# Fewer single blocks and earlier pairs in an on-chip-routed mixture of experts, with separately anchored scatters

## The chip, the core and the metric

The kernel runs on one core of a Trainium2 chip. Its engines are named as in the profile: PE is TensorE (PEld its weight loads), DVE is VectorE, ACT is ScalarE, POOL is GpSimd, and SP is the engine whose queue issues most loads. The metric is device time in microseconds. A run is given as the median of several executions.

## What is computed

28,672 tokens of 192 channels (8 sequences of 3,584) first go through a causal convolution with 7 taps, whose softmaxed weights are shared by the 24 channels of a head. The result then goes through a mixture of 8 experts with one expert per token. A token takes the expert with the largest logit, or, if its local gate is not below one half, the expert of the token before it.

```
w = softmax(weight)                                   # 8 heads x 7 taps
y[b, s, h] = sum_k w[h, k] * x_pad[b, s + k, h]       # 24 channels per head
logits = y @ w_gate ; local = sigmoid(y @ w_local)
e[s] = argmax(logits[s]) if s == 0 or local[s] < 0.5 else e[s - 1]
out[s] = softmax(logits[s])[e[s]] * (relu(y[s] @ w1[e[s]]) @ w2[e[s]])   # 192 -> 1024 -> 192
```

## The kernel before

**Parts and blocks.** Tokens come in 16 parts of 1,792. For each part, DVE (with eight ACT instructions) convolves, `route` finds each token's expert and place, and POOL scatters the 14 row groups of the part into the DRAM table `slots`, sorted by expert (`put`, L794, its indirect DMA on L801). A unit is 128 such rows of one expert. PE works through blocks of one unit (a single), two units (a pair) or four (a quad), always of one expert, since the 1.5 MB of that expert's weights are loaded once per block. Quads use a seven-product scheme (`seven`, L1136) and can only be formed when all parts are routed.

**The static plan.** How many blocks of each kind exist is fixed when the program is written, from what must be full whatever the routing. `ONE` counts singles after each part up to `EARLY` (L47, 3), `TWO` counts pairs after each later part up to `PAIRED` (L65, 60). With these values there are 35 singles (7 after the first part, 14 more after the second, 14 more after the third), then 60 pairs (3 after the fourth part, 7 more after each part that follows), then 13 quads, 4 pairs and 14 singles. In the loop over blocks (L1359) they run in this order. A spare group behind a conditional takes what is left over.

**A block.** `hidden` (L988) writes the hidden layer to `hps` (L999) and ACT takes it out with a relu (L1004). `turn` (L964) transposes the next block's rows on PE and ACT copies them out (L985). `output` (L1009) multiplies by the second weights into two PSUM tiles `yps` (L1016); ACT scales one half out (L1024), DVE adds the other half (L1030), and POOL scatters each unit's 128 finished rows to the output (L1034). `yps` has two buffers and a block uses both, so the next block's `output` can only begin when this block's L1030 is done.

**The order of the work between.** All engines work in the order of the program text as it is emitted. DVE's convolution and routing is cut into small pieces, and `step(time)` (L1258) emits pieces until their noted costs add up to `time`: routing pieces first, and convolution pieces (0.6 each, L411) from a "hop" on, which is where the next routing piece waits for another engine. A single has steps of 2.1, 1.2 and 1.3 around its output, a pair 4.8, 1.2 and 3.6. `start_conv` (L1229) lets a convolution begin if it is at most two parts ahead of the routing and no scatters of three parts before are left.

**Scatters and rows.** `put(behind)` takes one row group off the list `to_put` and ties its scatter to the instruction given. A single or a pair places two in `hidden`. A pair places one more behind the transposes while more than 7 are left, and one in `output` while more than 12 are left. `ensure(i)` (L1311), called at the head of block i, loads the rows of the blocks up to i + 3. A block of part g can only be loaded when all of g's scatters are emitted. While some are left, it does this:

```
while st["routed"] < g or any(p[0] <= g for p in to_put):
    if j > i + 2:
        return
    step(4.2)
    put()
```

Of the kernel before, what the change touches and what calls it, by code (L numbers as in the profile page):

```python
# [9 lines left out]
I32 = mybir.dt.int32  # L10
Act = mybir.ActivationFunctionType
# [6 lines left out]
P = 128  # L18
B, S, D = 8, 3584, 192
# [3 lines left out]
N = B * S  # L23
UT = 128
NT = 14
# [10 lines left out]
KD = D // DR  # L36
FK = F // P
BT = 2 * UT
KT = BT // P
# [4 lines left out]
CAP = CAPU * UT  # L44
NU = (N + E * (UT - 1)) // UT
DUMMY = E * CAPU
EARLY = 3  # L47
SPARE = 2


def _sure(tokens, size):

    return max(0, -(-(tokens - E * (size - 1)) // size))
# [3 lines left out]
def _likely(tokens, size, left):  # L57
# [4 lines left out]

LAST = NPART - 1
PADS = NPART
PAIRED = 60  # L65
LEFT4 = E * (QT // 2 + UT // 8)
LEFT2 = E * (BT // 2 + UT // 8)
ONE = [_sure(min(g + 1, EARLY) * PT, UT) for g in range(NPART)]
TWO = [min(PAIRED, _sure((g + 1) * PT - ONE[-1] * UT, BT)) if g >= EARLY else 0
       for g in range(NPART)]  # L70
# [13 lines left out]
IX = DG - 1  # L84
# [3 lines left out]
WA = F * KD // 2  # L88
# [8 lines left out]
def bcast_mid(ap, n):  # L97

    return ap.rearrange("p (o a) -> p o a", o=1).to_broadcast([ap.shape[0], n, ap.shape[1]])
# [3 lines left out]
def kernel(  # L103
# [10 lines left out]
    nc = tc.nc  # L114
# [45 lines left out]
    with tc.tile_pool(name="scr", bufs=1) as scr:  # L160
        w = scr.tile([1, H, KC], F32, name="w")
# [164 lines left out]
    slot = early[:, (H + 4) * TB:(H + 4) * TB + UT]  # L326
# [6 lines left out]
    rows = cst.tile([Q, 2, Q], F32, name="rows")  # L333
# [18 lines left out]
    for zero in (rk, bk, mk, mc, tq):  # L352
# [8 lines left out]
                      in_=bcast_mid(pad, KQ))  # L361
# [15 lines left out]
    def halves():  # L377
        return [(half, slice(half * DR, (half + 1) * DR)) for half in range(2)]
# [410 lines left out]
    to_put = []  # L789
    puts = []  # L790
    waited = set()
    SYNC = mybir.DependencyInfo(mybir.DependencyClass.Sync, mybir.DependencyReason.DATA)

    def put(behind=None):  # L794


        if not to_put:
            return
        g, rows, to = to_put.pop(0)
        nc.gpsimd.nop()  # L800
        ins = nc.gpsimd.indirect_dma_start(  # L801
            out=slots[:, :], in_=rows, in_offset=None,
            out_offset=bass.IndirectOffsetOnAxis(ap=to, axis=0)).ins
        if behind is not None:
            tc.add_manual_dep(ins, behind.ins.name, SYNC, reason="scatters apart")
        if puts:
            tc.declare_no_dep(ins, group="puts", reason="slots of their own")
        if g:
            tc.declare_no_dep(ins, group="gets", reason="those slots were full before")
        puts.append((g, ins))  # L810
        tc.add_to_no_dep_group("puts", ins)
        tc.add_to_no_dep_group(f"puts{g}", ins)
# [175 lines left out]
    def hidden(n, wb, xT, shares=(1, 1)):  # L988
        hT = hp.tile([P, FK, BT], F32, name="hT")
        w = slice(0, n * P)  # L990


        for two in range(2):
            hps = [hps_p.tile([P, 2, BT], F32, name="hps") for half in range(2)]
            for d in range(KD):
                for j in range(2):
                    f0 = (d * 4 + two * 2 + j) * P
                    for half, rows in halves():
                        nc.tensor.matmul(hps[half][:, j, w], lhsT=wb[rows, f0:f0 + P],  # L999
                                         rhs=xT[rows, d, w], start=(d == 0 and j == 0),  # L1000
                                         stop=(d == KD - 1), skip_group_check=True)
            for half in range(2):
                m = half * 4 + two * 2
                relu = nc.scalar.activation(hT[:, m:m + 2, w], hps[half][:, :, w], Act.Relu)  # L1004
            for _ in range(shares[two] if n == KT else (0, sum(shares))[two]):
                put(relu)
        return hT

    def output(n, wb, xg, hT):  # L1009

        yps = [yps_p.tile([P, 512], F32, name="yps") for half in range(2)]
        for m4 in ([0, 1, 4, 5], [2, 3, 6, 7]):
            for k in range(n):
                for m in m4:
                    for half, rows in halves():
                        nc.tensor.matmul(yps[half][:, k * D:(k + 1) * D],  # L1016
                                         lhsT=hT[rows, m, k * P:(k + 1) * P],
                                         rhs=wb[rows, WA + m * D:WA + (m + 1) * D],
                                         start=(m == 0 and k == 0), stop=(m == FK - 1),
                                         skip_group_check=True)  # L1020
        o_sb = op.tile([P, KT, D], F32, name="o_sb")
        y = [[yps[half][:, k * D:(k + 1) * D] for half in range(2)] for k in range(n)]
        for k in range(n):
            half = nc.scalar.activation(o_sb[:, k, :], y[k][0], Act.Copy, scale=xg[:, k, 0:1])  # L1024
        if n == KT and len(to_put) > NT - 2:
            put(half)

        step(1.2 if n > 1 or st["block"] else 0)
        for k in range(n):
            nc.vector.scalar_tensor_tensor(o_sb[:, k, :], y[k][1], xg[:, k, 0:1], o_sb[:, k, :],  # L1030
                                           Alu.mult, Alu.add)

            nc.gpsimd.nop()
            sent = nc.gpsimd.indirect_dma_start(  # L1034
                out=out, in_=o_sb[:, k, :], in_offset=None,
                out_offset=bass.IndirectOffsetOnAxis(ap=xg.bitcast(I32)[:, k, IX:], axis=0),
                bounds_check=N - 1, oob_is_err=False)
            tc.declare_no_dep(sent.ins, group="sent", reason="each token has one slot")
            tc.add_to_no_dep_group("sent", sent.ins)


    room = {}
# [215 lines left out]
    def step(time):  # L1258

        start_route()  # L1260
        start_conv()
        go = st["rgen"] is not None
        while time > 0:
            c = route_op() if go else conv_op()
            if c is None:
                if not go:
                    break
                go = False
            elif c == "hop":
                go = False  # L1270
            elif c == "placed":
                pass
            else:
                time -= c
# [10 lines left out]
    def rest(work):  # L1285
        for _ in work:
            pass
# [62 lines left out]
    xT, _ = turn(blocks[0][1], xgs[0])  # L1350
# [8 lines left out]
    for i, (_, n, _, _) in enumerate(blocks):  # L1359
        st["block"] = i  # L1360
        ensure(i)
        weights(i + AHEAD)
        if i == LATE:
            x_in[3] = load_x(3)
        if i == FIRST - 1:
            make_room()
        n_next = blocks[i + 1][1] if i + 1 < len(blocks) else 0

        def weights_next():
            return combine_w(wbs[i + 1]) if n_next == KQ else iter([None] * 4)  # L1370

        if i < FIRST:
            hT = hidden(n, wbs[i], xT, (1, 1) if i else (0, 0))
            if i < FIRST - 1:
                xT, copied = turn(n_next, xgs[i + 1])
                if len(to_put) > NT // 2 and n == KT:
                    put(copied)
            else:
                wt = list(weights_next())[-1]
                xT, _ = turn_in(n_next, turn_out(n_next, xgs[i + 1]))  # L1380
                xc = combine_x(xT)
            step(2.4 if i == 0 else 2.1 if n == 1 else 4.8)
            output(n, wbs.pop(i), xgs.pop(i), hT)
            if i == 0:
                rest(route1)
            step(1.3 if n == 1 else 3.6)
            continue
        if i == FIRST:
            banks.close()
            for k in range(3):  # L1390
                late_p.append(ctx.enter_context(tc.tile_pool(name=f"late{k}", bufs=1, space=PSUM)))

        def turn_next():
            return turn_out(n_next, xgs[i + 1]) if n_next else None

        if n == KQ:
            hT, at, wt = seven(wbs[i], wt, xT, xc, turn_next, weights_next)
        else:
            hT = hidden_late(n, wbs[i], xT)
            at = turn_next()  # L1400
        if n_next:
            xT, _ = turn_in(n_next, at)
        wts, xcs = [], []

        def rows_next():
            if n_next == KQ:
                xcs.append(combine_x(xT))
            if n == KQ:
                wts.append(next(wt))

        def between(part, two, k, ins):
            if n == KQ and part == 0 and two != k:
                put(ins)
                if k:
                    next(wt)

        output_late(n, wbs.pop(i), xgs.pop(i), hT, rows_next, between)
        if n == KQ:
            wt = wts[0]
        xc = xcs[0] if xcs else None  # L1420
# [89 lines left out]
```

## Time and profile before

| | |
|---|---|
| three runs | 1322.0, 1322.66, 1323.66 us; median 1322.66 |
| profiled execution | 1305.35 us, of which its span 1303.6 us |
| granted PE clock, mean | 0.997 |
| DVE busy | 846.3 us (65%), nearly all of it before 830 us |
| POOL busy | 523.1 us (40%) |
| wb weight loads of 1.5 MB | 122, besides 12 of a third of that |
| last routing result of parts 3, 4, 5 and 16 (DVE, L769) | 104.85, 161.7, 218.5 and 829.6 us |
| first pair's hidden layer (PE) | 252.5 us |

A line of the chain of waits gives start, length and what ran. A line of the timeline gives start, length, engine, line, operation and tiles, and in brackets how long the engine was idle before and what released it. In the list of waits, the numbers are the total, how often, and the longest. A row of windows gives the busy time of each engine in a stretch and its PE clock.

### The profile page before, as it was taken

The page shows a single profiled execution, that of the slowest core. Times are in us where ns is not written, and L with a number is a line of the kernel's source. Part 1 is how long each engine was busy: PE and PEld are TensorE (multiplying, and loading weights), DVE is VectorE, ACT ScalarE, POOL GpSimd, SP SyncE. Part 2 cuts the span into 40 slices and gives each one's busy share as a digit, 9 for nine tenths or more (in the row PEclk, how much of TensorE's full clock was granted, in tenths as well). Part 3 has the DMA queues.
Part 4 walks back from the last instruction along what each step waited for, and adds up shares of the span by engine and source line. Part 5 has one row for each costly group of instructions (what it writes and reads, how often), then busy time and mean ns, then how long its engine had stood idle before and what let it go on. Part 6 is the DMA issues. An engine that isn't in the chain of part 4 may idle for free.

```text
span 1303.6 us, 40830 instructions
## 1 busy us (share of the span) xinstructions
PE 1284.2 (99%) x16434; PEld 1220.6 (94%) x16434; DVE 846.3 (65%) x2526; ACT 651.1 (50%) x1482; POOL 523.1 (40%) x577
## 2 busy tenths in 40 slices
PE   9899999999999999999999999999999999999997
PEld 7799999999999999999999999999999999999997
DVE  5989898988988899998999996801333333330000
ACT  5456565544445445444454544444645556454453
POOL 3455353533435344353544534454433433322211
PEclk9999999999999999999999999999999999999999
DMA  5799999975757576575765755666323323324584
GB/s 195 285 357 415 386 384 345 398 273 202 269 203 278 196 274 244 207 280 190 281 246 204 281 193 205 214 213 235 128 87 135 122 105 140 110 94 167 212 303 164
DMA packets 63077, 300.42 MB, mean 230 GB/s; under 512 B 12064, under 2 KB 34263, under 8 KB 45474
## 3 DMA queue, kind: packets, MB, share of 16 engines
q1 hardware_dynamic: 40560, 252.54, 53.2%
q0 software_dynamic: 22320, 45.22, 9.5%
q8 instruction: 131, 2.15, 0.7%
q14 instruction: 64, 0.52, 0.1%
q10 hardware_dynamic: 2, 0.00, 0.0%
HBM read 252.12 MB, written 46.07 MB: 229 GB/s over the span
## 4 chain that ended last, share of the span: by engine, by line
PE 96%; DVE 3%; issue 0%; POOL 0%; POOLq 0%; ACT 0%; DVEq 0%
PE yps L1016 31%; PE hps L999 31%; PE ps L1196 15%; PE ps L1152 8%; PE ps L1103 4%; PE xps L383 2%; PE xps L1152 2%; PE hps L604 2%; DVE y_sb L411 1%; PE hps L233 1%; PE hps L178 0%; DVE hot L574 0%; PE hps L256 0%; PE yps L264 0%; DVE run L475 0%
## 5 line engine op out<-in xcount | busy, mean ns | idle before, releaser
L1016 PE MATMUL yps<-wb,hT 64*128 64x192 f32 x4960 | 429.8, 325 | 3.2 <-DVE o_sb L1030 2.4
L999 PE MATMUL hps<-xT,wb 64*128 64x256 f32 (+1 forms) x4560 | 425.9, 338 | 1.9 <-DVE at L503 1.2
L999 PEld LDWEIGHTS hps<-xT,wb 64*128 64x128 f32 x4560 | 378.7, 188 | 33.9 <-issue 3.9
L1016 PEld LDWEIGHTS yps<-wb,hT 64*128 64x128 f32 x4960 | 405.7, 187 | 4.6 <-DVE o_sb L1030 2.7
L411 DVE SCALAR_TENSOR_TENSOR y_sb<-x_sb,c,y_sb 128x336 f32<-128x336 f32 x672 | 375.6, 569 | 28.4 <-ACT y_sb L401 10.5
L801 POOL DMA_INDIRECT slots<-y_sb,posi x228 | 229.6, 1007 | 205.7 <-ACT xT L985 90.8
L1004 ACT ACTIVATE hT<-hps 128x512 f32<-128x512 f32 (+1 forms) x380 | 176.4, 516 | 244.5 <-PE hps L999 244.5
L1034 POOL DMA_INDIRECT out_dram<-o_sb,xg x155 | 161.5, 1042 | 276.0 <-DVE o_sb L1030 222.2
L1209 DVE SCALAR_TENSOR_TENSOR o_sb<-ps,y_sb,o_sb 128x192 f32<-128x192 f32 x74 | 28.1, 413 | 233.5 <-ACT o_sb L1206 233.5
L1214 POOL DMA_INDIRECT out_dram<-o_sb,y_sb x74 | 76.4, 1032 | 237.5 <-DVE o_sb L1209 218.7
L1196 PE MATMUL ps<-wb,x_sb 64*128 64x192 f32 x1952 | 165.0, 323 | 0.0
L1196 PEld LDWEIGHTS ps<-wb,x_sb 64*128 64x128 f32 x1952 | 159.3, 187 | 0.6
L1024 ACT ACTIVATE o_sb<-yps,xg 128x192 f32<-128x192 f32 x155 | 58.7, 418 | 178.4 <-PE yps L1016 178.3
L985 ACT COPY xT<-xps 128x256 f32<-128x256 f32 (+3 forms) x380 | 142.0, 374 | 10.6 <-PE xps L383 4.8
L1030 DVE SCALAR_TENSOR_TENSOR o_sb<-yps,xg,o_sb 128x192 f32<-128x192 f32 x155 | 58.6, 410 | 77.2 <-ACT o_sb L1024 77.0
L1206 ACT ACTIVATE o_sb<-ps,y_sb 128x192 f32<-128x192 f32 x74 | 27.9, 418 | 102.2 <-PE ps L1196 97.7
L1152 PE MATMUL ps<-x_sb,wb 64*128 64x256 f32 x624 | 73.7, 376 | 0.0
L1152 PEld LDWEIGHTS ps<-x_sb,wb 64*128 64x128 f32 x624 | 59.0, 187 | 7.3
L401 ACT ACTIVATE y_sb<-x_sb,c 128x336 f32<-128x336 f32 x112 | 61.9, 578 | 0.0
L1103 PE MATMUL ps<-x_sb,wb 64*128 64x128 f32 (+1 forms) x864 | 61.6, 295 | 0.0
L1103 PEld LDWEIGHTS ps<-x_sb,wb 64*128 64x128 f32 x864 | 59.4, 188 | 0.9 <-issue 0.2
L1083 ACT COPY x_sb<-xps 128x128 f32<-128x128 f32 (+5 forms) x124 | 58.7, 473 | 2.3
(277 smaller groups left out, 1043.5 us busy)
## 6 DMA issues: line engine op xcount, KB each, us to landing
wb<-in_w_dram SPq DMA_DIRECT2D x122, 1536.0 KB
x_sb<-in_x_dram SPq DMA_DIRECT2D x14, 1920.0 KB
xg<-slots SPq DMA_DIRECT2D x60, 195.0 KB
wb<-in_w_dram SPq DMA_DIRECT2D x12, 512.0 KB
y_sb<-slots SPq DMA_DIRECT2D x13, 390.0 KB
slots<-y_sb,posi POOLq DMA_INDIRECT x228
xg<-slots SPq DMA_DIRECT2D x33, 97.5 KB
x_sb<-in_xb_dram SPq DMA_DIRECT2D x4, 768.0 KB
```

Of the source, the lines that this page charges most:

```text
L401: nc.scalar.activation(cols(h), chans(h, 0), Act.Copy, scale=c[:, h, 0:1])
L411: nc.vector.scalar_tensor_tensor(cols(h), chans(h, k), c[:, h, k:k + 1], cols(h), Alu.mult, Alu.add)
L801: ins = nc.gpsimd.indirect_dma_start(out=slots[:, :], in_=rows, in_offset=None, out_offset=bass.IndirectOffsetOnAxis(ap=to, axis=0)).ins
L985: copied = nc.scalar.copy(a, b)
L999: nc.tensor.matmul(hps[half][:, j, w], lhsT=wb[rows, f0:f0 + P], rhs=xT[rows, d, w], start=(d == 0 and j == 0), stop=(d == KD - 1), skip_g ...
L1004: relu = nc.scalar.activation(hT[:, m:m + 2, w], hps[half][:, :, w], Act.Relu)
L1016: nc.tensor.matmul(yps[half][:, k * D:(k + 1) * D], lhsT=hT[rows, m, k * P:(k + 1) * P], rhs=wb[rows, WA + m * D:WA + (m + 1) * D], start= ...
L1034: sent = nc.gpsimd.indirect_dma_start(out=out, in_=o_sb[:, k, :], in_offset=None, out_offset=bass.IndirectOffsetOnAxis(ap=xg.bitcast(I32)[ ...
L1103: nc.tensor.matmul(hps[:, half, j, :], lhsT=wb[rows, f0:f0 + P], rhs=xT[rows, d, :], start=(d == 0 and j == 0), stop=(d == KD - 1), skip_g ...
L1152: ins = nc.tensor.matmul(to[:, half, j, :], lhsT=b[rows, j * P:(j + 1) * P], rhs=a[rows, :], start=(first and j == 0), stop=True, skip_gro ...
L1196: ins = nc.tensor.matmul(yps[:, half, k * D:(k + 1) * D], lhsT=h[two][rows, side, j, k * P:(k + 1) * P], rhs=wb[rows, WA + f * D:WA + (f + ...
L1214: sent = nc.gpsimd.indirect_dma_start(out=out, in_=o_sb[:, k, :], in_offset=None, out_offset=bass.IndirectOffsetOnAxis(ap=xg.bitcast(I32)[ ...
```

## The change

`EARLY` becomes 2 and `PAIRED` 63. By the plan's formulas that gives 21 singles (7 and 14), then 63 pairs (3 after the third part, then 7 after each), 15 quads, 4 pairs and 14 singles. The number of units worked on stays 229.

In `hidden`, a single's two scatters are placed one behind each half instead of both behind the second. In `output`, the extra scatter of a pair is tied to a matmul in the middle of the output instead of to the ACT instruction after it. The scatter of a block's second unit is no longer emitted in `output` but kept in a list `held` and emitted in the next block's `hidden`, tied to a matmul there, or, before the first quad, without a tie.

```diff
-EARLY = 3
+EARLY = 2
-PAIRED = 60
+PAIRED = 63
...
                     for half, rows in halves():
-                        nc.tensor.matmul(hps[half][:, j, w], lhsT=wb[rows, f0:f0 + P],
+                        ins = nc.tensor.matmul(hps[half][:, j, w], lhsT=wb[rows, f0:f0 + P],
...
+                        if held and d:
+                            held.pop(0)(ins)
...
-            for _ in range(shares[two] if n == KT else (0, sum(shares))[two]):
+            for _ in range(shares[two]):
                 put(relu)
...
+                if m4[0] and k == 0 and n == KT and len(to_put) > NT - 2:
+                    put(ins)
...
-        if n == KT and len(to_put) > NT - 2:
-            put(half)
...
+            if k == 0:
+                deliver(o_sb, xg, 0)
+            else:
+                held.append(lambda ins, k=k: deliver(o_sb, xg, k, ins))
+
+    held = []
+
+    def deliver(o_sb, xg, k, behind=None):
+
+        nc.gpsimd.nop()
+        sent = nc.gpsimd.indirect_dma_start(
+            out=out, in_=o_sb[:, k, :], in_offset=None,
...
+        if behind is not None:
+            tc.add_manual_dep(sent.ins, behind.ins.name, SYNC, reason="scatters apart")
...
         if i == FIRST:
+            while held:
+                held.pop(0)(None)
```

More of the change, by code (lines that the diff above doesn't have):

```diff
@@ L998, in hidden @@
                     for half, rows in halves():
-                        nc.tensor.matmul(hps[half][:, j, w], lhsT=wb[rows, f0:f0 + P],
-                                         rhs=xT[rows, d, w], start=(d == 0 and j == 0),
-                                         stop=(d == KD - 1), skip_group_check=True)
+                        ins = nc.tensor.matmul(hps[half][:, j, w], lhsT=wb[rows, f0:f0 + P],
+                                               rhs=xT[rows, d, w], start=(d == 0 and j == 0),
+                                               stop=(d == KD - 1), skip_group_check=True)
+                        if held and d:
+                            held.pop(0)(ins)
             for half in range(2):
@@ L1015, in output @@
                     for half, rows in halves():
[L1016 to L1020, printed above, removed]
+                        ins = nc.tensor.matmul(yps[half][:, k * D:(k + 1) * D],
+                                               lhsT=hT[rows, m, k * P:(k + 1) * P],
+                                               rhs=wb[rows, WA + m * D:WA + (m + 1) * D],
+                                               start=(m == 0 and k == 0), stop=(m == FK - 1),
+                                               skip_group_check=True)
+                if m4[0] and k == 0 and n == KT and len(to_put) > NT - 2:
+                    put(ins)
         o_sb = op.tile([P, KT, D], F32, name="o_sb")
@@ L1023, in output @@
         for k in range(n):
-            half = nc.scalar.activation(o_sb[:, k, :], y[k][0], Act.Copy, scale=xg[:, k, 0:1])
-        if n == KT and len(to_put) > NT - 2:
-            put(half)
+            nc.scalar.activation(o_sb[:, k, :], y[k][0], Act.Copy, scale=xg[:, k, 0:1])
         step(1.2 if n > 1 or st["block"] else 0)
@@ L1031, in output @@
                                            Alu.mult, Alu.add)
[L1033 to L1039, printed above, removed]
+            if k == 0:
[7 more added lines that the diff above has]
+            out=out, in_=o_sb[:, k, :], in_offset=None,
+            out_offset=bass.IndirectOffsetOnAxis(ap=xg.bitcast(I32)[:, k, IX:], axis=0),
+            bounds_check=N - 1, oob_is_err=False)
+        if behind is not None:
+            tc.add_manual_dep(sent.ins, behind.ins.name, SYNC, reason="scatters apart")
+        tc.declare_no_dep(sent.ins, group="sent", reason="each token has one slot")
+        tc.add_to_no_dep_group("sent", sent.ins)
     room = {}
```

## The prediction, written before the changed kernel ran

> **What bounds the kernel now.** I read the page first: engines, then slices.
>
> ```profile
> PE 1284.2 (99%) x16434; PEld 1220.6 (94%) x16434; DVE 846.3 (65%) x2526; ACT 651.1 (50%) x1482; POOL 523.1 (40%) x577
> ...
> DVE  5989898988988899998999996801333333330000
> ```
>
> PE is never free for long. DVE is nearly full for the first 24 slices (782 us) and mostly at a third or less after 850 us, so only before that can DVE work push PE. The chain of waits gives each kind of block its period, from one block to the next of its kind.
>
> ```profile
> 98.16 2.68 PE hps L999 x48
> 103.61 2.68 PE hps L999 x48
> 109.05 2.68 PE hps L999 x48
> ...
> 263.47 5.18 PE hps L999 x48
> ...
> 274.13 5.18 PE hps L999 x48
> ...
> 284.80 5.18 PE hps L999 x48
> ...
> 961.25 10.40 PE ps L1196 x128
> ...
> 981.68 10.40 PE ps L1196 x128
> ...
> 1002.09 10.40 PE ps L1196 x128
> ```
>
> A single takes (109.05 - 98.16)/2 = 5.445 us, a pair (284.80 - 263.47)/2 = 10.665, a quad (1002.09 - 961.25)/2 = 20.42. Per unit: 5.445, 5.333, 5.105.
>
> The list of PE's waits and DVE's timeline then show the one way in which DVE stops PE.
>
> ```profile
> PE yps L1016 <- DVE o_sb L1030: 2.4, 1, 2.4
> ```
>
> ```profile
> 59.51 4.68 DVE L411 SCALAR_TENSOR_TENSOR y_sb<-x_sb,c,y_sb 128x336 f32<-128x336 f32 x8
> 64.10 0.41 DVE L1030 SCALAR_TENSOR_TENSOR o_sb<-yps,xg,o_sb 128x192 f32<-128x192 f32 x1
> 64.43 5.34 DVE L411 SCALAR_TENSOR_TENSOR y_sb<-x_sb,c,y_sb 128x336 f32<-128x336 f32 x9
> ```
>
> ```profile
> 64.00:72.00 8.00, 7.43 (x88) 7.43 (x90) 7.65 (x16) 1.94 (x6) 4.01 (x4) 0.79 1.04 411
> ```
>
> Early on, convolution pieces stand ahead of an output's L1030 on DVE, and the next output waits for its PSUM tiles. The last row is the windows' row for 64 to 72 us: the clock after that stop is 0.79, so (1 - 0.79) x 8 = 1.7 us more are lost.
>
> Last, the timelines of DVE and POOL give the third convolved part's dates (the fourth of all, index 3).
>
> ```profile
> 161.74 0.17 DVE L769 CAST posi<-pos 128x14 int32<-128x14 f32 x1
> ```
>
> ```profile
> 164.26 0.96 POOL L801 DMA_INDIRECT slots<-y_sb,posi  x1 [1.18 <-ACT xT L985]
> ...
> 198.32 0.96 POOL L801 DMA_INDIRECT slots<-y_sb,posi  x1 [0.30 <-issue]
> ```
>
> Its 14 scatters go out over seven singles, two each. Before, its first block is block 35, at 252.5 us: 53 us to spare.
>
> [...] L1030 runs only after the eight pieces ahead of it. [...] here SP issues the first quad's rows at 885.76, 2.6 us after the last needed scatter ended on POOL (882.21 + 0.96), and I use 2.6.
>
> **Part 1, the plan.** 14 singles go, 3 pairs and 2 quads come: -14 x 5.445 + 3 x 10.665 + 2 x 20.42 = -76.23 + 32.00 + 40.84 = -3.4 us of PE. Nine weight loads fewer are worth nothing: in SP's own waits, L940 waits for PE (558 us in all), so loads wait for buffers, not PE for loads. Whether the 15 quads fill is settled by the reference's inputs: counting experts with its seed, the table rules fill all 15 quads and 4 pairs, and 14 singles are left. So the spare group does not run, as before.
>
> **Part 2, when part index 3 is needed.** I followed `step`, `put` and `ensure` block by block, adding noted costs. For the kernel before this puts index 2's places after block 8's output and index 3's after block 18's, as the trace does (104.85 follows block 8's L1030, 161.74 block 18's). Blocks 0 to 20 are singles in both kernels, so this holds after the change. Blocks 19 and 20 place two scatters each; 10 are left. Block 21 is now a pair of index 2 and places 2 + 1; 7 are left. Block 24 is the first of index 3. At block 21, `ensure` may return (24 > 23). At block 22 it may not: it emits seven times `step(4.2)` and `put()`, ahead of block 22's own work on every engine.
>
> These seven steps hold: 7 convolution pieces; 5 more, which end part 4; the 4 transposes of routing 4 and 3 pieces of part 5; 7 pieces, with the logits' matmuls; routing to L653; two small ones and 7 pieces; routing from L667 to L720. The 29 pieces cost 5.28/9 = 0.587 each in the trace: 17.0 us. The routing is read off its first run on DVE (81.05 to 99.86 us, outputs left out): 3.15 + 5.24 + 0.24 + 4.7 = 13.3. Sum: 30.3 us.
>
> **Part 3, what that does to PE.** Time zero is the end of block 21's L1030. DVE then has block 21's last step (6 pieces, 3.5), the 30.3, and block 22's own 4.8 and 1.2 (routing, about 6.2) before block 22's L1030: it starts at 40.0. Normally it starts 9.9 after (10.665 less 0.74 for two adds), so it is 30.1 late. PE has a cushion: a next output normally starts 4.76 after the L1030 (263.95 to 268.71), and needs only the two adds and about 0.1: 3.9 us. PE loses 30.1 - 3.9 = 26.2.
>
> The stop falls in two. First, logits 4 stand before block 22's `hidden` in PE's order and wait for their transposes, at 3.5 + 4.1 + 2.9 + 3.15 = 13.7. Then `output` of 22 and `hidden` of 23 run, and `output` of 23 waits for block 22's adds, to 40.9. The relus of 22 stand behind routing 4's exponential on ACT, near 23, inside the same wait. The first stop's cold clock also lies inside it. The second comes after about 5 us of idling, so I add the 1.7 us: 27.9 in all.
>
> Nothing gives it back: DVE is ahead afterwards, but PE lacks nothing then. The seven untied scatters take 7 x 1.27 = 9 us of POOL after block 21's first output scatter; with 2.6 to land, index 3's rows load from about 13, long before block 23 turns them.
>
> At the first quad, one scatter of the last part is left at block 82 and its step is empty (routing is over): nothing, as its rows are needed 16 us later.
>
> **Part 4, the anchors.** The same number of scatters (about 1 us of POOL each) is tied elsewhere. A second unit's scatter waits for a matmul of the next `hidden`, about 1 us after the output ends, when its own add is ending too. Queued behind it are scatters only; who waits is `o_sb`, two blocks later. Zero. Marking matmuls: quads with tied scatters (910.40 to 930.82) and without (981.68 to 1002.09) take 20.42 and 20.41; zero, bounds -1 and +2.
>
> **Sum.** -3.4 + 26.2 + 1.7 + 0 = +24.5 us, on the profiled 1305.35: 1329.9. The runs' median lies 17.3 above the profiled execution, a difference I keep: 1347.2, which I round to 1347.
>
> **Rivals.**
> - *The other side: DVE never gets between.* If no scatter of index 3 were left at block 22, only part 1 remains: 1322.66 - 3.4 = 1319.3. For it: PE waits on DVE once in the whole trace. Against it: it decides at seven scatters, and 14 less 2 + 2 + 3 leaves seven. If I misread `ensure` or the count, this is the time.
> - *The steps run dry.* If part 5 may not begin, 17 of its pieces (10 us) are not there: PE loses 16.2, and 1322.66 + 14.5 = 1337.2. Against it: routing is at 3, and 5 is at most two ahead.
> - *A longer stop.* If routing in one stretch takes a fifth longer on DVE (36 instead of 30) and the clock stays low through `output` and `hidden` (10.5 us at half speed, 5.2 lost instead of 1.7): 1347.2 + 6 + 3.5 = 1356.7. For it: the row for 64 to 72 us is one case only.
> - The change does what it says in any case: the plan is plain arithmetic.
>
> **Chances.** The forced stop as worked out 0.74 (own range 1341 to 1353), no stop 0.12, dry 0.08, longer 0.06. What can be told from no change is 0.2%, 2.6 us. The no-stop case lies just beyond it, so I give 0.10 to faster, 0.03 to the same, 0.87 to slower. From 1336 to 1354 the range takes in the dry case and leaves out the no-stop and longer ones.
>
> **What will show it.** PE with two gaps near 190 to 230 us, of some 15 and 5 us, the second ended by L1030; DVE without a break through them; seven L801 in a row on POOL; the PE clock low after each gap; single, pair and quad periods unchanged; PE's end about 24 us later. I am wrong if PE is as dense there as before, if the seven scatters are spread out, or if quads change their period.

## The result, and the profile after

| | kernel before | changed kernel |
|---|---|---|
| first comparison (four runs of each) | 1323.16 us | 1342.44 us, ratio 1.0139 [1.0113, 1.0166] |
| a later comparison (11 and 5 runs) | 1305.63 us | 1326.49 us, ratio 1.0164 [1.0149, 1.0179] |

The change makes the kernel slower, by 19.3 us in the first comparison and by 20.9 in the later one. The forecast was 1347 us, 24.5 over the kernel before. These differences are between medians; the ratios are taken over the single runs, so the quotient of two medians differs from them by up to 0.0007.

The page of the changed kernel, engines and slices:

```profile
PE 1293.8 (97%) x16082; PEld 1244.9 (93%) x16082; DVE 857.1 (64%) x2523; ACT 650.3 (49%) x1416; POOL 528.2 (39%) x585
...
PE   9899977999999999999999999999999999999997
DVE  6878889898989999999899886313333333330000
...
PEclk9999998999999999999999999999999999999999
```

PE has fewer matmuls than before, yet two slices at 7, between 168 and 235 us, and the one slice with a lower clock is there too. The hole shows best in PE's timeline (start, length, engine, line, tiles, count; in brackets the idle time before it and what ended it). L1006 is the relu, L1018 the output's matmul, L1032 DVE's add: each two lines further down than before.

```profile
185.97 5.42 PE L1018 MATMUL yps<-wb,hT 64*128 64x192 f32 x64
204.47 1.41 PE L604 MATMUL hps<-z,wg 64*32 64x128 f32 x8 [13.08 <-DVE z L594]
206.09 2.66 PE L604 MATMUL hps<-z,wg 64*32 64x128 f32 x88 [0.22 <-DVE z L594]
208.68 5.45 PE L999 MATMUL hps<-xT,wb 64*128 64x256 f32 x48
217.42 7.15 PE L1018 MATMUL yps<-wb,hT 64*128 64x192 f32 x64 [3.06 <-ACT hT L1006]
224.41 5.35 PE L999 MATMUL hps<-xT,wb 64*128 64x256 f32 x48
233.38 5.30 PE L1018 MATMUL yps<-wb,hT 64*128 64x192 f32 x61 [3.02 <-DVE o_sb L1032]
```

Three waits, 13.08, 3.06 and 3.02 us. The first stands before block 22's hidden layer, where the logits of routing 4 wait for their transposes (L594). The second is block 22's output, whose relus stand on ACT behind the exponential of that routing. The third is block 23's output, which waits for the adds of block 22. For the second, ACT's timeline has the exponential (L662), which waited 6.42 us for DVE, and the relus right behind it:

```profile
216.59 0.30 ACT L662 ACTIVATE ex<-ex 128x112 f32<-128x112 f32 x1 [6.42 <-DVE eq L637]
216.79 2.04 ACT L1006 ACTIVATE hT<-hps 128x512 f32<-128x512 f32 x4
```

DVE's timeline for the same stretch shows what it does meanwhile:

```profile
191.87 0.74 DVE L1032 SCALAR_TENSOR_TENSOR o_sb<-yps,xg,o_sb 128x192 f32<-128x192 f32 x2 [1.98 <-ACT o_sb L1028]
192.53 10.78 DVE L411 SCALAR_TENSOR_TENSOR y_sb<-x_sb,c,y_sb 128x336 f32<-128x336 f32 x18
203.34 3.16 DVE L594 STREAM_TRANSPOSE z<-y_sb 128x768 f32<-128x768 f32 x4
206.42 5.86 DVE L411 SCALAR_TENSOR_TENSOR y_sb<-x_sb,c,y_sb 128x336 f32<-128x336 f32 x10
...
217.55 4.07 DVE L411 SCALAR_TENSOR_TENSOR y_sb<-x_sb,c,y_sb 128x336 f32<-128x336 f32 x7
...
230.98 0.18 DVE L769 CAST posi<-pos 128x14 int32<-128x14 f32 x1
232.58 0.74 DVE L1032 SCALAR_TENSOR_TENSOR o_sb<-yps,xg,o_sb 128x192 f32<-128x192 f32 x2
```

Only the first line has a bracket: after block 21's adds DVE is never idle until block 22's adds begin, 39.97 us after the first pair of adds ended (232.58 - 191.87 - 0.74). PE's holes are DVE's work, not DVE's waits. On POOL the seven scatters follow each other, some 1.3 us apart. The next one, at 210.52, is that of block 21's second unit: it is tied to a matmul of block 22's hidden layer, which begins at 208.68, so it comes late with PE (the releaser in its bracket is inferred). Block 22's own first output scatter follows its adds, at 233.28, when the seven are long over:

```profile
193.86 1.30 POOL L801 DMA_INDIRECT slots<-y_sb,posi  x1 [0.31 <-issue]
195.46 0.96 POOL L801 DMA_INDIRECT slots<-y_sb,posi  x1 [0.30 <-issue]
...
202.02 0.96 POOL L801 DMA_INDIRECT slots<-y_sb,posi  x1 [0.31 <-issue]
210.52 0.98 POOL L1045 DMA_INDIRECT out_dram<-o_sb,xg  x1 [7.54 <-DVE y_sb L411]
...
233.28 0.98 POOL L1045 DMA_INDIRECT out_dram<-o_sb,xg  x1 [0.38 <-DVE o_sb L1032]
```

After the hole PE is dense. The chain of waits shows quads as long as before, (1007.10 - 966.26) / 2 = 20.42:

```profile
966.26 3.45 PE ps L1165 x32
...
986.68 3.45 PE ps L1165 x32
...
1007.10 3.45 PE ps L1165 x32
```

One thing in this trace was not foreseen. In PE's list of waits the relu (L1006) stands with twelve waits:

```profile
PE hps L604 <- DVE z L594: 13.3, 2, 13.1
PE yps L1018 <- ACT hT L1006: 9.0, 12, 3.1
PE yps L1018 <- DVE o_sb L1032: 4.2, 2, 3.0
```

One of the twelve is the 3.06 above; the others are singles, nine of them between 99 and 150 us, whose output waits in its middle for the second relu, as here:

```profile
124.37 1.57 PE L1018 MATMUL yps<-wb,hT 64*128 64x192 f32 x16 [0.56 <-ACT hT L1006]
```

Such a single takes up to 6.3 us instead of 5.445. Whether that is the change's doing was the first question for the experiments.

### The profile page after: what moved, and what is told of

It is laid out like the page before. It is cut to its first block, busy times and chain, and to the rows that moved or that the text cites. A ratio compares the mean times of both kernels' runs of the same rounds, so it can differ in the third digit from the quotient of the medians.

```text
span 1340.4 us, 39961 instructions
## 1 busy us (share of the span) xinstructions
PE 1293.8 (97%) x16082; PEld 1244.9 (93%) x16082; DVE 857.1 (64%) x2523; ACT 650.3 (49%) x1416; POOL 528.2 (39%) x585
## 4 chain that ended last, share of the span: by engine, by line
PE 92%; DVE 5%; ACT 1%; issue 1%; another core or an unknown queue 1%; POOL 0%; POOLq 0%; DVEq 0%; ACTq 0%
PE yps L1018 27%; PE hps L999 27%; PE ps L1209 16%; PE ps L1165 9%; PE ps L1116 4%; PE xps L383 3%; DVE y_sb L411 2%; PE xps L1165 2%; PE hps L604 2%; PE hps L233 1%; ACT hT L1006 0%; PE hps L178 0%; DVE hot L574 0%; PE yps L580 0%
## 5 line engine op out<-in xcount | busy, mean ns | idle before, releaser
L1018 PE MATMUL yps<-wb,hT 64*128 64x192 f32 x4704 | 415.8, 327 | 15.7 <-ACT hT L1006 9.0
L1018 PEld LDWEIGHTS yps<-wb,hT 64*128 64x128 f32 x4704 | 386.7, 188 | 24.8 <-ACT hT L1006 12.4
L999 PE MATMUL hps<-xT,wb 64*128 64x256 f32 (+1 forms) x4032 | 403.8, 351 | 1.9 <-DVE at L503 1.2
L999 PEld LDWEIGHTS hps<-xT,wb 64*128 64x128 f32 x4032 | 363.7, 187 | 26.3 <-issue 3.9
L1006 ACT ACTIVATE hT<-hps 128x512 f32<-128x512 f32 (+1 forms) x336 | 164.9, 541 | 264.9 <-PE hps L999 140.5
L1209 PE MATMUL ps<-wb,x_sb 64*128 64x192 f32 x2144 | 181.8, 323 | 0.0
L1209 PEld LDWEIGHTS ps<-wb,x_sb 64*128 64x128 f32 x2144 | 176.0, 187 | 0.2 <-issue 0.2
L1032 DVE SCALAR_TENSOR_TENSOR o_sb<-yps,xg,o_sb 128x192 f32<-128x192 f32 x147 | 55.0, 409 | 68.0 <-ACT o_sb L1028 54.4
L1165 PE MATMUL ps<-x_sb,wb 64*128 64x256 f32 x720 | 87.0, 376 | 0.0
L1165 PEld LDWEIGHTS ps<-x_sb,wb 64*128 64x128 f32 x720 | 77.7, 187 | 0.0
L1096 ACT COPY x_sb<-xps 64x512 f32<-64x512 f32 (+6 forms) x132 | 64.2, 487 | 2.5
L1116 PEld LDWEIGHTS ps<-x_sb,wb 64*128 64x128 f32 x864 | 60.0, 188 | 1.1 <-ACT o_sb L1219 0.8
```

The source lines that it names most:

```text
L999: ins = nc.tensor.matmul(hps[half][:, j, w], lhsT=wb[rows, f0:f0 + P], rhs=xT[rows, d, w], start=(d == 0 and j == 0), stop=(d == KD - 1), ...
L1018: ins = nc.tensor.matmul(yps[half][:, k * D:(k + 1) * D], lhsT=hT[rows, m, k * P:(k + 1) * P], rhs=wb[rows, WA + m * D:WA + (m + 1) * D], ...
L1096: copied = nc.scalar.copy(a, b)
L1116: nc.tensor.matmul(hps[:, half, j, :], lhsT=wb[rows, f0:f0 + P], rhs=xT[rows, d, :], start=(d == 0 and j == 0), stop=(d == KD - 1), skip_g ...
L1165: ins = nc.tensor.matmul(to[:, half, j, :], lhsT=b[rows, j * P:(j + 1) * P], rhs=a[rows, :], start=(first and j == 0), stop=True, skip_gro ...
L1209: ins = nc.tensor.matmul(yps[:, half, k * D:(k + 1) * D], lhsT=h[two][rows, side, j, k * P:(k + 1) * P], rhs=wb[rows, WA + f * D:WA + (f + ...
```

## The experiments

Theory S, that of the prediction: the seven forced steps at block 22 make the change slower, the plan itself saves 3.4 us, and the new ties are worth nothing. Rival A: the new ties cost, by the late second relus. Rival B: the ties bring something, which hides part of the stop. Rival C: the stop is made by the seven scatters, or by the row loads behind them, not by DVE's work.

### The kernel before, once more (e1 and e8)

No edit.

> The kernel before, unchanged, profiled once more. Question: is the profiled 1305.35 us an ordinary execution, or do the timed ones (1322 to 1329) lose about 17 us somewhere that its trace does not show? Theory S (the forced steps at block 22 alone make the change slower): this trace, at an execution of about 1322, already has in its singles the late second relu that the changed kernel's trace has (about 0.5 to 0.7 us at a dozen singles, some 8 us before block 21), and other losses like it; part index 3 is then routed (L769) at about 170 us rather than at 161.74. Rival A (the anchors make it): the singles keep 5.445 us, L769 of index 3 stands at about 162 us, and the second relu is late only in the changed kernel.

> The kernel before, profiled beside the changed one. If this chip is one on which the kernel before takes about 1322 us, as in the first times: theory S expects the late second relu of the singles in this trace too (index 3 routed at about 170 us), so that it is the chip's and not the change's. If the chip is one of 1305 us, the singles keep 5.445 us in both kernels.

e1 took 1305.46 us (12 runs), e8 1304.83 (one run): these runs, and all that follow, on three chips, met the time of the profiled execution and not the 1323 of the first comparison. In e1's trace PE's list of waits has no relu among its lines, and its singles keep their period. So e1's expectation for theory S, a second relu that is late in the kernel before too, was not met; nor was rival A's, since the changed kernel in the same place (e5, below) has none either. PE's list of waits there:

```profile
PE hps L604 <- DVE z L594: 13.1, 2, 12.9
PE yps L1018 <- DVE o_sb L1032: 5.0, 2, 3.0
PE yps L1018 <- ACT hT L1006: 3.1, 1, 3.1
```

The three waits of the stop are there to 0.2 us, and the late relus of the singles are gone. So the code alone doesn't make them. What made them in that first trace, and whether the 1323 us of the kernel before hold the same, isn't known: there is no trace of the kernel before at 1323 us.

### The plan alone, and the ties alone (e2, e3), and the whole change again (e5)

e2 is the kernel before with `EARLY = 2` and `PAIRED = 63`. e3 is the changed kernel with these two set back:

```diff
-EARLY = 2
+EARLY = 3
-PAIRED = 63
+PAIRED = 60
```

> 21 singles and 63 pairs, with the scatters placed as before. Block 22 still finds seven scatters left and emits seven steps. Theory S: as slow as the whole change, 23 to 26 us over the kernel before if the terms were right (-3.4 + 26.2 + 1.7), about 19 if one of them was too large by five. Rival A (the anchors cost, the plan does not): within 5 us of the kernel before. Rival B (the anchors gave back five of the 24.5): about 24 to 25 us over, and thus some 5 us slower than the whole change.

> 35 singles and 60 pairs as before, with the new placing and tying of scatters. No forced steps anywhere. Theory S: within 2 us of the kernel before. Rival A: slower by 8 us or more (12 or more singles with a second relu about 0.7 us late). Rival B: faster by about 5 us.

> The changed kernel as it is, on the same chip as the next three runs. The plan alone cost 23.8 us and the anchors alone 0.7 in the runs before, so theory S expects about 24 us over the kernel before of the same chip (1.0175 to 1.0195). Rival B (plan and anchors together cost less than their sum): 19 us as in the first comparison (1.0139 to 1.015).

| | median | kernel before | ratio |
|---|---|---|---|
| e2, plan alone | 1328.59 | 1304.79 | 1.0176 [1.0162, 1.0190] |
| e3, ties alone | 1305.47 | 1304.79 | 1.0003 [0.9995, 1.0012] |
| e5, both | 1326.49 | 1305.63 | 1.0164 [1.0149, 1.0179] |

The plan alone is as slow as the whole change, and the ties alone are worth nothing that can be measured. Rival A falls. Of rival B a part stays open. By the medians e2 lies 2.9 us further over its kernel before than e5; the intervals of the two overlap, but leave room for some 4 us that the ties could give back in company with the plan. e5 came out at 20.9, three less than expected and between the two forecasts.

### Without the forced steps (e4)

```diff
             while st["routed"] < g or any(p[0] <= g for p in to_put):
                 if j > i + 2:
                     return
-                step(4.2)
+                if st["routed"] < g:
+                    step(4.2)
                 put()
```

> The whole change, but in ensure a step is made only while the part is not routed; where only scatters are left, they are emitted without one. At block 22 seven scatters follow each other with no DVE work between. Theory S: 26 to 28 us faster than the changed kernel, that is 1314 to 1318 us, some 3 to 8 us faster than the kernel before. Rival C (the stop is not the steps but the row loads, which wait for the seven scatters in a row, or POOL's queue of scatters ahead of the outputs): 5 us or less is gained over the changed kernel. Rival A: the two gaps at block 22 go, but 8 us or more over the kernel before stay.

1308.62 us, ratio 1.0027 [1.0013, 1.0040]: 3.8 us over the kernel before, where 3 to 8 under it were expected. Against the changed kernel 17 are gained (20.9 - 3.8, each against its own kernel before), where 26 to 28 were expected. The seven scatters stand in a row here too, and PE's timeline at block 22 is without a wait:

```profile
186.37 5.25 PE L1018 MATMUL yps<-wb,hT 64*128 64x192 f32 x62
...
191.62 5.34 PE L999 MATMUL hps<-xT,wb 64*128 64x256 f32 x47
...
197.03 5.42 PE L1018 MATMUL yps<-wb,hT 64*128 64x192 f32 x63
202.38 1.59 PE L604 MATMUL hps<-z,wg 64*32 64x128 f32 x96
203.90 5.45 PE L999 MATMUL hps<-xT,wb 64*128 64x256 f32 x48
```

So rival C falls: same scatters, same loads, no stop. The missing 7 us (from -3.4 to +3.8) are in another place. This kernel's PE has a wait of a length that no other run shows at the first quad (e6 has 0.58 there, the rest none):

```profile
863.06 1.12 PE L383 MATMUL xps<-ident,y_sb 64*128 64x64 f32 x16 [5.37 <-DMA y_sb<-slots]
```

POOL's timeline shows why. After the output scatter at 843.02 it runs eleven scatters of the last part, and only then may SP load the quad's rows (it does at 859.74):

```profile
844.31 0.96 POOL L801 DMA_INDIRECT slots<-y_sb,posi  x1 [0.30 <-issue]
...
856.95 0.96 POOL L801 DMA_INDIRECT slots<-y_sb,posi  x1 [0.30 <-issue]
```

The matmuls behind this wait are longer: the rows' transposes take 1.12 us where e7's, below, take 0.64, and the output behind them 7.62 where e7's takes 5.43. So the first quad takes 16.1 us to the next one where e7's takes 13.5; that this is the clock is inferred from these lengths alone. The wait and these 2.6 us are 8.0, and 7.9 is what e7 gains over e4, each against its own kernel before.

The last routing result (L769) comes at 825.3 us here and at 819.6 in e2, but PE is at its first quad 20 us sooner than in e2 (863.1 against 883.8). By program order, eleven scatters are left at block 82, where the changed kernel has one. In the changed kernel the forced steps had done 30 us of DVE's work while PE stood, and that lead is what its last rows lived on.

### The last part's scatters sooner (e7, e9)

e7 is e4 with more scatters in the last pairs; e9 is the same with the ties of the kernel before.

```diff
-            hT = hidden(n, wbs[i], xT, (1, 1) if i else (0, 0))
+            share = 0 if i == 0 else 3 if i >= FIRST - 6 else 1
+            hT = hidden(n, wbs[i], xT, (share, share))
```

> The whole change without forced steps (as e4), and with three scatters instead of one behind each half of the last six pairs, so that one scatter of the last part is left at block 82 instead of eleven. Theory S: of the 7.3 us by which e4 missed -3.4, 5.4 are PE's wait for the first quad's rows behind eleven scatters in a row, and the rest is the clock after it. Both go: 3 to 4 us faster than the kernel before (0.9970 to 0.9980), that is 7 us faster than e4. Rival E (the 7 us are in the pairs or quads, or the scatters crowd the outputs on POOL instead): 2 us or less better than e4.

> As e7 (new plan, no forced steps, three scatters behind each half of the last six pairs), but with the ties of the kernel before: a single's scatters both behind its second half, a second unit's output scatter right after its add, the extra scatter of a pair behind ACT. Theory S (the ties are worth nothing): within 2 us of e7, that is 2 to 5 us faster than the kernel before. Rival B (the new ties bring something as soon as the stop is gone): 3 us or more slower than e7.

e7 took 1301.51 us beside 1305.63, ratio 0.9969 [0.9958, 0.9980]: 4.1 us faster than the kernel before, as expected, and faster than both. SP's and PE's timelines of e7 at the first quad:

```profile
851.26 1.20 SPq L947 DMA_DIRECT2D y_sb<-slots  x2
```

```profile
859.29 0.64 PE L383 MATMUL xps<-ident,y_sb 64*128 64x64 f32 x16
```

The rows are asked for 8 us before PE turns them, and PE waits for nothing. More scatters in the last pairs were not tried in the kernel before; its PE has no wait for a quad's rows, so no such wait was there to be saved. e9 took 1302.70, ratio 0.9981 [0.9972, 0.9990], within 2 us of e7 as expected: the ties are not what makes e7 fast. Beside the plan they may be worth a little: e9's PE has a wait for the rows of block 24 that e7 doesn't have. There block 21's second output scatter goes out on POOL ahead of the seven, and in e7 behind them:

```profile
197.92 0.45 PE L383 MATMUL xps<-ident,xg 64*128 64x64 f32 x8 [1.73 <-DMA xg<-slots]
```

### How the stop grows with the work in it (e6, e10)

In e6 the forced steps of the changed kernel are halved, `step(2.1)`; in e10 e7 gets forced steps of `step(1.2)` back.

> The whole change, but each forced step may only place work of 2.1 instead of 4.2. The steps then place 14.2 of noted cost instead of 29.1, about 14.8 us of DVE instead of 30.3. Theory S (PE loses what DVE does beyond a cushion of 3.9 us): L1032 of block 22 is 14.6 us late instead of 30.1, PE loses 10.7 instead of 26.2 and 1.7 for the clock; with -3.4 for the plan that is 9 us over the kernel before, up to 11 if the first quad's rows come up to 2 us late. Rival C (the stop comes from seven scatters or row loads, not from the steps' work): still 20 us or more. Rival D (each stop has a fixed price, in restart and clock, of 5 us or more): 14 us or more.

> As e7, but with forced steps of 1.2: at block 22 they hold only the 12 pieces left of part 4, 7.0 us of DVE. Theory S as the prediction had it (only the adds of block 22 count, with a cushion of 3.9 us): PE loses 3.1 us, up to 1.7 more for the clock; with -3.4 that is 0 to 1.5 us over the kernel before. Theory S2, after e6 (every PE instruction that needs DVE's work counts, and the logits' matmuls are one, with no such cushion): routing 4 starts in block 22's own step, behind these 12 pieces, the transposes are ready 0.7 + 3.5 + 7.0 + 3.15 = 14.4 us after block 21's L1032 begins, PE comes to the logits about 5.1 us after it and waits 9, and loses 2 to 4 more to the clock: 8 to 10 us over the kernel before, with a PE wait of some 9 us on DVE's z.

e6 took 1320.38 us, ratio 1.0112 [1.0094, 1.0129]: 14.8 us over the kernel before instead of 9 to 11. PE's timeline says what was left out in the expectation:

```profile
194.57 1.41 PE L604 MATMUL hps<-z,wg 64*32 64x128 f32 x8 [12.90 <-DVE z L594]
196.20 3.23 PE L604 MATMUL hps<-z,wg 64*32 64x128 f32 x88 [0.22 <-DVE z L594]
199.36 6.33 PE L999 MATMUL hps<-xT,wb 64*128 64x256 f32 x48
205.75 5.42 PE L1018 MATMUL yps<-wb,hT 64*128 64x192 f32 x64
```

The waits for the relu and for the adds are gone, as less work in the steps should have it, but the wait of the logits is as long as ever: halving the steps leaves the same 18 pieces of convolution ahead of the transposes, as e6's DVE shows:

```profile
182.65 10.76 DVE L411 SCALAR_TENSOR_TENSOR y_sb<-x_sb,c,y_sb 128x336 f32<-128x336 f32 x18
```

From block 21's hidden layer to block 25's, e4 and e7 take 44.6 us, e6 61.7: 17.1 lost. Of these, 13.1 are waits and the rest is the clock, 0.50 and 0.60 in the windows from 194 to 202 us: the logits, 1.5 us at full speed (e4, 202.38 to 203.90), take 4.8 here with 0.2 of waiting in it, and the hidden layer behind them 0.9 more than in e4. With -3.4 that is 13.7, and 14.8 was measured. Rival C asked for 20 or more and falls. Rival D asked for 14 or more and met it, but not by its mechanism: it is not a fixed price, as e10 shows with a smaller one, but a second consumer of DVE's work with a deadline of its own.

e10 took 1309.17 us, ratio 1.0030 [1.0019, 1.0041]: 3.5 us over the kernel before, between the two forecasts, so neither was met. PE's timeline:

```profile
188.46 5.42 PE L1018 MATMUL yps<-wb,hT 64*128 64x192 f32 x63
196.11 0.41 PE L604 MATMUL hps<-z,wg 64*32 64x128 f32 x4 [2.24 <-DVE z L594]
196.88 0.41 PE L604 MATMUL hps<-z,wg 64*32 64x128 f32 x4 [0.36 <-DVE z L594]
197.74 3.13 PE L604 MATMUL hps<-z,wg 64*32 64x128 f32 x88 [0.45 <-DVE z L594]
```

The logits stand after block 22's output here and not before it, so S2's 9 us didn't come. They wait 2.24 + 0.36 + 0.45 = 3.05 us. That is the 3.1 of theory S (7.0 us of DVE less a cushion of 3.9), but at another instruction than the one whose cushion was worked out, so the closeness may be chance. From block 21 to 25 the loss is 50.0 - 44.6 = 5.4, so the clock, 0.67 in the window from 198 to 202 us, took 2.4 instead of the 1.7. In this kernel forced steps come at block 29 too (3.7 of noted cost), which the expectation hadn't counted; of the next pairs two take 0.4 and 1.1 us more than their like in e7. From block 21 to the first quad e10 takes 6.9 us more than e7, and -3.4 + 6.9 = 3.5.

## Why the prediction was right

**The plan, -3.4.** Held: with the stop and the late rows gone, e7 is 4.1 us faster, interval 2.6 to 5.5. Quads keep 20.42.

**The seven steps and what they hold.** Held to the piece. 18 pieces, 4 transposes, 10 and 7 pieces stand between the two L1032, in the order of the program text (the 18 are the six of block 21's last step and twelve of the 29; the other seventeen are 3 + 7 and 7). Predicted was a start of block 22's adds 40.0 us after the end of block 21's; it was 39.97.

**PE loses 26.2.** The place, the order of the waits and their cause held: e4 takes the steps away and the stop is gone, with all else in place. The size was somewhat large. From block 21 to block 25, PE takes 44.6 us without the stop, 68.6 in e5, 70.3 in the first trace and 70.7 in e2: losses of 24.1, 25.7 and 26.2, against 27.9 with the clock. Two terms of the sum are off. The logits' matmuls run inside the stop, and elsewhere they would have lengthened a pair, by 1.6 us (12.3 against 10.7 in e7); the prediction took 26.2 without giving that back, which would have been 24.6. And the 1.7 for the clock, the author's estimate from one stop of the kernel before (2.41 us of waiting, then 0.79 over 8 us), was counted after the third wait, which was foreseen as some 5 us and is 3.02: the output after it took 5.30 us, not longer than its usual 5.42. In e2 PE stood about 4.7 us there, by its windows from 218 to 226 us, and the clock was 0.50 and 0.85 in the two windows from 222 us on: by these about 3.12 x 0.50 + 4 x 0.15 = 2.2 us, so there the 1.7 was due. In e5, -3.4 + 24.1 = 20.7, and 20.9 was measured. Two of the signs in the list were not met as named: there are three gaps and not two, since the wait for the relus, which was counted inside the second gap, stands by itself with 3.06 us; and the clock is not low after the last one (in the first trace 0.75 in the window from 206 to 210 us, behind the first gap, 0.57 from 218 to 222, behind the second, and 1.00 from 234 to 238, behind the third). The first leaves the sum as it is, because block 22's adds set when the last gap ends; the second is the 1.7 above.

**Nothing gives it back.** Wrong in its reason, though it cost the forecast nothing. Within the changed kernel the lead that DVE gains is not idle: it keeps the last scatters ahead of the first quad. Taking away the stop alone brings 17 us, not 24, as e4 shows; e7 brings the rest.

**What DVE does to PE in the kernel before.** The prediction reads that PE waits on DVE once in the whole trace. Its list of PE's waits has six on DVE. The other five, 3.8 us in all, come before 48 us and are for other results of DVE (L475, L503, L574), not for an output's adds. So the reading is wrong, but only the case for a rival rested on it.

**The ties, 0.** Held alone (e3), to about 2 us. In company with the plan it is shown to some 4 us only: over the kernel before, e2 lies 2.9 us above e5 and e9 1.2 above e7, both on the side of a small gain by the ties and both within the noise.

**The 17.3 us between profile and runs.** Keeping it as a constant is what put the forecast near 1342: the changed kernel, too, takes 16 us more in the first comparison than in the later one. No line of the profile before said what these 17.3 us are or that the changed kernel would have them too, so this part of the forecast was luck; the 24.5 was worked out step by step from the profile and the program. The first trace has 9.8 of the 16.6 us between the two spans before block 21, mostly in singles with late relus; the cause stays open. Because of it one sign in the list was not met in the first trace, that singles keep their period; in e5 they do.

**The rivals.** *DVE never gets between* is e4 by another way, and shows that 1319.3 was too good for it: without the forced steps the last rows would have been late. *The steps run dry* falls by the 17 pieces that are there. *A longer stop* falls: block 22's adds began when foreseen, so routing took no longer. The half speed that it supposes does occur in the kernel before: its windows of 1 us show 0.50 from 66 to 69 us, behind the stop of 2.41 us.

## What to carry to other kernels

A loop that catches up on a late dependency should place only what that dependency lacks: here the scatters were ready, and the steps between them did work for later parts in front of work due now. For work put ahead on an engine that runs it in program order, as DVE ran 18 pieces (10.78 us) ahead of the transposes here, look for every consumer in the order of time, not for the last one alone: halving it may leave the first stop whole. And when a stall goes, ask what the stalled time was used for elsewhere; the engine that was not stopped had been gaining a lead, and the next deadline may have lived on it.

## What the runs showed of the hardware that was not expected

- Waits of the same length left different clocks behind them. In e5, the output after a wait of 3.10 us took 7.15 us, with a clock of 0.80 and 0.78 in its windows; the one after a wait of 3.03 us, 16 us later, took 5.30 at 1.00. Why they differ is not shown by any run here. These are the windows of e5 from 206 us on (PE busy, then the other engines; the clock is the third number from the right):

```profile
206.00:210.00 4.00, 2.40 (x20) 2.40 (x22) 3.68 (x14) 3.20 (x8) 0.00 (x0) 0.80 0.00 0
210.00:214.00 4.00, 4.00 (x42) 4.00 (x40) 3.71 (x15) 0.62 (x2) 0.00 (x0) 0.78 0.00 0
...
222.00:226.00 4.00, 2.44 (x30) 2.44 (x32) 3.65 (x21) 1.15 (x3) 2.92 (x3) 1.00 0.89 355
```

- After the wait of 12.9 us the clock came back later than the 1.7 us of loss suggest: in e6, with 0.50 and 0.60 in the windows from 194 to 198 and 198 to 202 us, the logits and the hidden layer behind them took 3.1 and about 0.9 us longer than in e4, waits left out. It differs from run to run: after the same wait these two windows show 0.50 and 0.76 in e2, and 0.50 and 0.98 in e5, which lost 2.4 us there.
- The same program took 1.2 to 1.3% longer in one set of runs than in another (1323 and 1305 us for the kernel before, 1342 and 1326 for the changed one), with a mean clock of 0.991 and 0.990 in the two traces of the changed kernel. The intervals of the two ratios overlap (1.0139 [1.0113, 1.0166] and 1.0164 [1.0149, 1.0179]); absolute times do not agree.
